# Linear attention and a gated feed-forward on one core: the queries' projections in two PSUM banks of their own, their third pass queued behind the next group's first, two stacked operands

## The chip, the cores and the metric

The kernel runs on one core of a Trainium2 chip. The metric is the device time of one launch in microseconds (us). Lower is better. The times before are the median of three runs, and one further execution was recorded by the hardware profiler.

The core's engines are called as the profile calls them: PE (TensorE, matrix products; PEld is its weight loader), DVE (VectorE), ACT (ScalarE), POOL (GpSimd) and SP (SyncE, which here only issues DMAs). Each engine works through its own list of instructions in the order in which they stand there, and an instruction that has to wait holds back all that stand behind it on that engine.

## The reference

```python
def phi(x):                                   # x: (8, 8, 576, 64), w_phi: (64, 128)
    proj = np.einsum('bhsd,df->bhsf', x, w_phi)
    proj = proj - np.max(np.abs(proj), axis=-1, keepdims=True)
    return np.concatenate([np.exp(proj), np.exp(-proj)], axis=-1)
q_p, k_p = phi(q), phi(k)
kv  = np.einsum('bhsf,bhsd->bhfd', k_p, v)
z   = np.sum(k_p, axis=2)
num = np.einsum('bhsf,bhfd->bhsd', q_p, kv)
den = np.einsum('bhsf,bhf->bhs', q_p, z)[..., None] + 1e-06
x   = num / den                               # heads side by side: (8, 576, 512)
h   = np.maximum(x @ w_in, 0.0)               # (8, 576, 1024)
conv = sum(conv_w[k] * shifted(h, k - 1) for k in range(3))
out = (h * sigmoid(conv)) @ w_out             # (8, 576, 512), all float32
```

## The kernel before

The eight batches are cut into two units each (four heads to a unit), and each unit into five groups of columns; group 0 has 128 columns of each of two heads, the others 256. Three kinds of process run through this list. A key process (`k_process`) projects a group of keys (PSUM tile `kp`), takes the largest absolute value and the exponentials, and adds the products with the values into `kv`. A query process (`q_process`) projects a group of queries (PSUM tile `qp`), takes the exponentials in both signs and multiplies them with `kv` (PSUM tile `nm`). The feed-forward process multiplies with `w_in` (`hp`), convolves, gates, and multiplies with `w_out` (`op`). A small planner at the end of the file steps these processes in turn. It decides in which order the instructions are traced; then a list scheduler, which holds a model of the engines, fixes each engine's list. The names in a list read as tile, batch, unit, group, and a running number: `qp5_0_1_6607` is the projection of batch 5, unit 0, group 1.

From batch 2 on a group of queries goes this way. Its columns are loaded by two DMAs on SP (`qr`, line 196). ACT copies them, rounded, into the stacked operand `qx` (line 199), and POOL puts the remainder into its lower half (line 200): rows 0 to 63 of `qx` are the rounded part, rows 64 to 127 the rest. PE makes a first and a second pass over `qx` into the PSUM tile `qp` (lines 353 and 354). The largest absolute value of each column is then found: by a reduction with a transpose on DVE (`qmt`, line 358), three small copies on ACT (line 361), and four small instructions on DVE (lines 365 to 369, `mx` and `qmp`). The negative maximum is brought back into two rows of `qx`, as a rounded part and its rest, by two DMAs on SP (line 371). A third pass on PE (line 378) subtracts it from `qp`. Only then can ACT take the two exponentials (line 387, `qe`), which free the bank of `qp`; the third pass is the last reader of `qx`, and frees its slot.

The first two batches go without the stack: their projections (line 220, also called `qp`) are normalised on DVE and turned by PE into the tile `tp` (line 346).

PSUM has eight banks here. The pool `pg` holds four under one tag `g`, which `qp`, `tp`, `kp` and `nm` share. The pool `pm` holds two (`hp`, `op`), and `pk` two for `kv`. A tile that asks for a bank waits until the last reader of an earlier tile is through: DVE's subtraction `ks` (line 230) for a `kp`, ACT's copies `num` (line 439) for an `nm`, ACT's exponentials for a `qp`. Of the stacked operand there are three slots (tag `qs`), of the tiles `num`, in which a unit's products are gathered, three. POOL also makes the keys' two parts (`kxh`, line 62, and `kxl`, line 65) and the first tap of the convolution (`c`, line 512).

Of the kernel before, what the change touches and what calls it, by code (L numbers as in the profile page):

```python
# [7 lines left out]
F32 = mybir.dt.float32  # L8
F32R = mybir.dt.float32r
# [3 lines left out]
ALU = mybir.AluOpType  # L13
AX = mybir.AxisListType.X

B, H, S, D = 8, 8, 576, 64
F = 128
DM, FF = 512, 1024
P = 128
# [3 lines left out]
VW = D + 1  # L23
# [12 lines left out]
def kernel(  # L36
# [150 lines left out]
    def load_split(src, b, qd, g, kind):  # L187
# [5 lines left out]
        if kind == "q":  # L193
            raw = sb.tile([P, 2, n * P], F32, name=f"qr{b}_{qd}_{g}", tag="qr", bufs=2)
            for h in range(2):
                nc.sync.dma_start(out=raw[D * h : D * h + D, :, :],
                                  in_=src[b, qd, :, c0 : c0 + n * P].rearrange("(i d) s -> d i s", d=D))
            x = sb.tile([P, 2, n * P], F32R, name=f"qx{b}_{qd}_{g}", tag="qs", bufs=3)
            nc.scalar.activation(out=x, in_=raw, func=AF.Copy)  # L199
# [9 lines left out]
    def project(n, hi, lo, b, qd, g, kind):  # L209

        if b == 0 and kind == "k":

            ps = pm.tile([P, n * 256], F32, name=f"{kind}p{b}_{qd}_{g}", tag="m")
        else:
            ps = pg.tile([P, n * 256], F32, name=f"{kind}p{b}_{qd}_{g}", tag="g", bufs=4)
        for t in range(n):
# [11 lines left out]
        nc.vector.tensor_reduce(out=m, in_=ps3, axis=AX, op=ALU.max, apply_absolute_value=True)  # L228
        pr = sb.tile([P, 2 * n, F], F32, name=f"{kind}s{b}_{qd}_{g}", tag=kind + "s", bufs=3 if kind == "q" else 2)
        nc.vector.tensor_tensor(out=pr, in0=ps3, in1=m.unsqueeze(2).broadcast_to([P, 2 * n, F]), op=ALU.subtract)  # L230
# [89 lines left out]
    den = {}  # L320
    numt = {}
    xh, xl = {}, {}

    def q_process(b, qd, g):
# [11 lines left out]
        if lo is None:  # L336
# [5 lines left out]

            tp = pg.tile([P, 2, n, P], F32, name=f"tp{b}_{qd}_{g}", tag="g", bufs=4)
            for t in range(n):
# [3 lines left out]
        else:  # L348
            x = hi
            tp = pg.tile([P, 2, n, P], F32, name=f"qp{b}_{qd}_{g}", tag="g", bufs=4)  # L350
            tpf, xf = tp.rearrange("p i t s -> p (i t s)"), x.rearrange("p i s -> p (i s)")
            c = w // 32
            nc.tensor.matmul(out=tpf, lhsT=wq_hi, rhs=xf, start=True, stop=False, skip_group_check=True)
            nc.tensor.matmul(out=tpf, lhsT=wq_lo, rhs=xf, start=False, stop=False, skip_group_check=True)

            mt = sb.tile([P, 4, 16], F32, name=f"qmt{b}_{qd}_{g}", tag="qmt", bufs=2)
            with tc.high_priority():
# [8 lines left out]
                nc.vector.tensor_reduce(out=m[:, 0:c], in_=mr, axis=AX, op=ALU.max)  # L366
                nc.vector.tensor_tensor(out=mp[:, 16 : 16 + c].bitcast(F32R), in0=m[:, 0:c], in1=mp[:, 0:c], op=ALU.subtract)
                mpt = sb.tile([32, 32], F32, name=f"qmp{b}_{qd}_{g}", tag="qmp", bufs=2)
                nc.vector.transpose(out=mpt, in_=mp)
                for i in range(2):  # L370
                    nc.sync.dma_start(out=xf[D + i : D + i + 1, :].bitcast(F32).rearrange("k (c t) -> k c t", t=32),
                                      in_=mpt[16 * i : 16 * i + c, :])
            yield pe(230 * n)
# [3 lines left out]
            with tc.high_priority():  # L377
                nc.tensor.matmul(out=tpf, lhsT=wq_m, rhs=xf, start=False, stop=True, skip_group_check=True)
            yield pe(115 * n)
# [15 lines left out]
        for pr_, _, _, _ in parts:  # L395
            if b > 0:
                yield until(("x", b - 1, qd * 2 + pr_, 1))
        ps = pg.tile([VW, 2, n * P], F32, name=f"nm{b}_{qd}_{g}", tag="g", bufs=4)
        ins = None
# [27 lines left out]
        for pr_, o, s0, w in parts:  # L427
            if (b, qd, pr_) not in den:
                den[b, qd, pr_] = sb.tile([72, 16], F32, name=f"den{b}_{qd}_{pr_}", tag="den", bufs=3)
                numt[b, qd, pr_] = sb.tile([P, S], F32, name=f"num{b}_{qd}_{pr_}", tag="num", bufs=3)  # L430
            dn, nt = den[b, qd, pr_], numt[b, qd, pr_]
# [271 lines left out]
```

## Time and profile before

| | |
|---|---|
| median of 3 runs | 848.88 us (848.18 to 851.27) |
| profiled execution | 846.93 us |
| its span, first to last instruction | 845.1 us |
| mean granted TensorE clock | 0.982 |
| PE busy | 784.7 us, 93% of the span |
| PEld busy | 746.8 us, 88% |
| DVE busy | 654.0 us, 77% |
| ACT busy | 637.9 us, 75% |
| POOL busy | 313.8 us, 37% |

The span is the time from the first instruction to the last, and what lies around it is 1.8 us. Busy time of an engine is the union of its instructions; matmuls overlap in the records, so that a PE row of 0.30 us can stand every 0.13 us. "Idle before" is the time in which the engine had nothing in it just before the instruction, and the name behind the arrow is the instruction that ended the wait.

### The profile page before, as it was taken

What the parts mean: (1) busy time and instruction counts of PE and PEld (TensorE: products, weight loads), DVE (VectorE), ACT (ScalarE), POOL (GpSimd) and SP (SyncE); (2) the same over time, 40 slices, a digit from 0 to 9 for tenths busy, and PEclk for the clock granted to TensorE, in tenths of its full rate; (3) what the DMA queues carried; (4) which work ended last, traced back from release to release, by engine and by line L of the source; (5) the groups of instructions that cost most, each with busy time, mean ns of one, the idle gap of its engine ahead of it and who ended that gap; (6) DMA issues with size and microseconds to landing.
All of it is one profiled execution on the core that took longest, in us unless ns stands there. A gap on an engine that the chain in (4) does not pass through costs nothing.

```text
span 845.1 us, 17785 instructions
## 1 busy us (share of the span) xinstructions
PE 784.7 (93%) x5972; PEld 746.8 (88%) x5972; DVE 654.0 (77%) x1570; ACT 637.9 (75%) x1468; POOL 313.8 (37%) x395
## 2 busy tenths in 40 slices
PE   7789789789989989998999999999989899999998
PEld 6678779789889979998999998998979889999998
DVE  6689997897887859887769887787868877766561
ACT  4689776979788788887889879799777978744332
POOL 5755564351533415334343342514515212211110
PEclk9999899999999999999999999999999999999999
DMA  5544322212121211222222322213212200000001
GB/s 167 159 135 136 115 77 55 83 30 81 55 85 44 84 40 51 71 70 71 69 78 55 88 55 86 56 47 92 57 48 58 73 21 11 22 30 29 23 15 50
DMA packets 68427, 56.49 MB, mean 67 GB/s; under 512 B 19440, under 2 KB 66288, under 8 KB 68336
## 3 DMA queue, kind: packets, MB, share of 16 engines
q1 hardware_dynamic: 68336, 55.36, 22.6%
q8 instruction: 48, 0.79, 0.4%
q14 instruction: 43, 0.35, 0.1%
HBM read 45.21 MB, written 9.44 MB: 65 GB/s over the span
## 4 chain that ended last, share of the span: by engine, by line
PE 54%; ACT 18%; DVE 13%; DMA 7%; issue 5%; SPq 2%; POOL 2%; ACTq 0%; DVEq 0%; POOLq 0%
PE op L548 16%; PE hp L489 16%; PE kv L279 7%; PE nm L416 6%; DVE c L517 3%; PE nm L408 2%; ACT qh L60 2%; ACT qe L387 2%; ACT num L439 2%; DVE ql L65 2%; ACT qx L199 1%; DMA qr<-in_qT_dram 1%; DMA w_r<-in_w_in_dram 1%; ACT c L521 1%; PE qp L220 1%
## 5 line engine op out<-in xcount | busy, mean ns | idle before, releaser
L512 POOL TENSOR_SCALAR c<-h,cw 128x288 f32<-128x288 f32 x128 | 87.4, 686 | 229.5 <-ACT h L496 192.9
L517 DVE SCALAR_TENSOR_TENSOR c<-h,cw,c 128x287 f32<-128x287 f32 (+1 forms) x256 | 138.5, 548 | 38.0 <-POOL c L512 36.5
L279 PE MATMUL kv<-v,ke 128*128 128x65 f32 x1024 | 159.4, 254 | 3.2 <-ACT ke L260 3.2
L279 PEld LDWEIGHTS kv<-v,ke 128*128 128x128 f32 x1024 | 154.2, 193 | 8.3 <-ACT ke L260 3.8
L489 PE MATMUL hp<-xh,win_hi 128*128 128x290 f32 x512 | 155.9, 306 | 3.6 <-ACT os L553 1.4
L489 PE MATMUL hp<-xl,win_hi 128*128 128x290 f32 x512 | 155.1, 303 | 0.0
L489 PE MATMUL hp<-xh,win_lo 128*128 128x290 f32 x512 | 154.3, 301 | 0.0
L548 PE MATMUL op<-gh,wout_hi 128*128 128x288 f32 x512 | 152.2, 298 | 0.5 <-ACT os L553 0.5
L548 PE MATMUL op<-gl,wout_hi 128*128 128x288 f32 x512 | 151.6, 296 | 0.0
L548 PE MATMUL op<-gh,wout_lo 128*128 128x288 f32 x512 | 151.4, 296 | 0.0
L200 POOL TENSOR_TENSOR qx<-qr,qx 64x512 fp32r<-64x512 f32 (+1 forms) x60 | 77.6, 1296 | 137.6 <-ACT qx L199 99.0
L65 DVE TENSOR_TENSOR ql<-qe,qh 128x512 fp32r<-128x512 f32 x112 | 92.3, 838 | 28.3 <-ACT qh L60 28.0
L489 PEld LDWEIGHTS hp<-xh,win_hi 128*128 128x128 f32 x512 | 98.3, 193 | 8.0 <-ACT os L553 3.3
L489 PEld LDWEIGHTS hp<-xl,win_hi 128*128 128x128 f32 x512 | 99.3, 194 | 1.2 <-DVE den L452 0.2
L489 PEld LDWEIGHTS hp<-xh,win_lo 128*128 128x128 f32 x512 | 99.1, 194 | 0.4
L548 PEld LDWEIGHTS op<-gh,wout_hi 128*128 128x128 f32 x512 | 96.2, 188 | 2.0 <-ACT os L553 1.2
L548 PEld LDWEIGHTS op<-gh,wout_lo 128*128 128x128 f32 x512 | 96.5, 188 | 0.3
L548 PEld LDWEIGHTS op<-gl,wout_hi 128*128 128x128 f32 x512 | 96.3, 188 | 0.5
L496 ACT ACTIVATE h<-hp 128x290 f32<-128x290 f32 x128 | 51.5, 407 | 38.4 <-PE hp L489 37.7
L62 POOL TENSOR_SCALAR kxh<-kr 128x256 fp32r<-128x256 f32 (+1 forms) x80 | 41.3, 518 | 103.1 <-PE kp L224 72.1
L416 PE MATMUL nm<-ql,kvh 128*65 128x256 f32 x224 | 68.8, 309 | 1.1 <-DVE ql L65 0.8
L416 PE MATMUL nm<-qh,kvh 128*65 128x256 f32 x224 | 62.6, 287 | 7.0 <-ACT num L439 4.4
(99 smaller groups left out, 1905.8 us busy)
## 6 DMA issues: line engine op xcount, KB each, us to landing
qr<-in_qT_dram SPq DMA_DIRECT2D x112, 128.0 KB
v<-in_vt_dram SPq DMA_DIRECT2D x80, 130.0 KB
out_dram<-os SPq DMA_DIRECT2D x64, 144.0 KB
kr<-in_kT_dram SPq DMA_DIRECT2D x64, 128.0 KB
w_r<-in_w_in_dram SPq DMA_DIRECT2D x8, 512.0 KB
w_r<-in_w_out_dram SPq DMA_DIRECT2D x8, 512.0 KB
rr<-rc SPq DMA_DIRECT2D x128, 2.2 KB
qr<-in_qT_dram SPq DMA_DIRECT2D x28, 64.0 KB
```

The lines of the kernel that those rows point to most:

```text
L60: nc.scalar.activation(out=hi, in_=src, func=AF.Copy)
L62: nc.gpsimd.tensor_scalar(out=hi, in0=src, scalar1=1.0, scalar2=0.0, op0=ALU.mult, op1=ALU.add)
L65: eng_lo.tensor_tensor(out=lo, in0=src, in1=hi.bitcast(F32), op=ALU.subtract)
L200: nc.gpsimd.tensor_tensor(out=x[D:P], in0=raw[D:P], in1=x[D:P].bitcast(F32), op=ALU.subtract)
L279: ins = nc.tensor.matmul(out=kp[i][:, s, p0 : p0 + VW], lhsT=lhsT, rhs=v[:, (2 * t + i) * VW : (2 * t + i + 1) * VW], start=False, stop=(g ...
L387: nc.scalar.activation(out=e, in_=tps, func=AF.Exp, scale=1.0 - 2.0 * s)
L416: ins = after(ins, lambda: nc.tensor.matmul(out=ps[:, i, o : o + w], lhsT=w_, rhs=x_, start=(k == 0), stop=(k == 5)))
L489: nc.tensor.matmul(out=ps, lhsT=w_, rhs=x_, start=(k == 0), stop=(k == 11))
L496: nc.scalar.activation(out=hs, in_=ps, func=AF.Relu)
L512: nc.gpsimd.tensor_scalar(out=cv, in0=hs[:, o : o + TC], scalar1=cw[:, f, 1:2], scalar2=0.0, op0=ALU.mult, op1=ALU.add)
L517: nc.vector.scalar_tensor_tensor(out=cv[:, lo:hi], in0=hs[:, o + j - 1 + lo : o + j - 1 + hi], scalar=cw[:, f, j : j + 1], in1=cv[:, lo:hi ...
L548: nc.tensor.matmul(out=ps, lhsT=w_, rhs=x_, start=(k == 0), stop=(k == 23))
```

## The change

Five edits go together. The four shared PSUM banks become two with the tag `gq`, which only the queries' `qp` and `tp` use, and two with the tag `g` for `kp` and `nm`. The third pass of a group is bound to stand behind the first pass of the next group in PE's list. This is an edge for the scheduler's order alone and adds no semaphore. The two rows of the maximum are laid side by side (`mp[:, c : 2 * c]` in place of `mp[:, 16 : 16 + c]`) and go in one DMA, not two. The slots with the tag `qs`, the stacked operands and the first batches' normalised projections, are two, not three. The tiles `num` are four, not three. The instructions of PE, DVE, ACT and POOL are the same in kind and number.

```diff
--- before.py
+++ after.py
@@ -195,7 +195,7 @@
             for h in range(2):
                 nc.sync.dma_start(out=raw[D * h : D * h + D, :, :],
                                   in_=src[b, qd, :, c0 : c0 + n * P].rearrange("(i d) s -> d i s", d=D))
-            x = sb.tile([P, 2, n * P], F32R, name=f"qx{b}_{qd}_{g}", tag="qs", bufs=3)
+            x = sb.tile([P, 2, n * P], F32R, name=f"qx{b}_{qd}_{g}", tag="qs", bufs=2)
             nc.scalar.activation(out=x, in_=raw, func=AF.Copy)
             nc.gpsimd.tensor_tensor(out=x[D:P], in0=raw[D:P], in1=x[D:P].bitcast(F32), op=ALU.subtract)
             return n, x, x
@@ -212,7 +212,7 @@
 
             ps = pm.tile([P, n * 256], F32, name=f"{kind}p{b}_{qd}_{g}", tag="m")
         else:
-            ps = pg.tile([P, n * 256], F32, name=f"{kind}p{b}_{qd}_{g}", tag="g", bufs=4)
+            ps = pg.tile([P, n * 256], F32, name=f"{kind}p{b}_{qd}_{g}", tag="gq" if kind == "q" else "g", bufs=2)
         for t in range(n):
             o = ps[:, t * 256 : (t + 1) * 256]
             his = hi[:, t * P : (t + 1) * P]
@@ -226,7 +226,7 @@
         ps3 = ps.rearrange("p (t f) -> p t f", f=F)
         m = sb.tile([P, 2 * n], F32, name=f"{kind}m{b}_{qd}_{g}", tag="m", bufs=4)
         nc.vector.tensor_reduce(out=m, in_=ps3, axis=AX, op=ALU.max, apply_absolute_value=True)
-        pr = sb.tile([P, 2 * n, F], F32, name=f"{kind}s{b}_{qd}_{g}", tag=kind + "s", bufs=3 if kind == "q" else 2)
+        pr = sb.tile([P, 2 * n, F], F32, name=f"{kind}s{b}_{qd}_{g}", tag=kind + "s", bufs=2)
         nc.vector.tensor_tensor(out=pr, in0=ps3, in1=m.unsqueeze(2).broadcast_to([P, 2 * n, F]), op=ALU.subtract)
         return pr
 
@@ -319,6 +319,13 @@
 
     den = {}
     numt = {}
+    firsts, third = {}, {}
+
+    def behind(ins, other):
+
+        tc.add_manual_dep(ins.ins, other.ins.name,
+                          mybir.DependencyInfo(mybir.DependencyClass.NoSync, mybir.DependencyReason.DATA),
+                          reason="a group's third pass behind the next group's first")
     xh, xl = {}, {}
 
     def q_process(b, qd, g):
@@ -340,17 +347,20 @@
             yield until(back("num", 2))
             set_ready(("tp", *divmod(j, 5)))
 
-            tp = pg.tile([P, 2, n, P], F32, name=f"tp{b}_{qd}_{g}", tag="g", bufs=4)
+            tp = pg.tile([P, 2, n, P], F32, name=f"tp{b}_{qd}_{g}", tag="gq", bufs=2)
             for t in range(n):
                 for i in range(2):
                     nc.tensor.transpose(out=tp[:, i, t, :], in_=pr[:, 2 * t + i, :], identity=idn)
             yield pe(220 * n)
         else:
             x = hi
-            tp = pg.tile([P, 2, n, P], F32, name=f"qp{b}_{qd}_{g}", tag="g", bufs=4)
+            tp = pg.tile([P, 2, n, P], F32, name=f"qp{b}_{qd}_{g}", tag="gq", bufs=2)
             tpf, xf = tp.rearrange("p i t s -> p (i t s)"), x.rearrange("p i s -> p (i s)")
             c = w // 32
-            nc.tensor.matmul(out=tpf, lhsT=wq_hi, rhs=xf, start=True, stop=False, skip_group_check=True)
+            first = nc.tensor.matmul(out=tpf, lhsT=wq_hi, rhs=xf, start=True, stop=False, skip_group_check=True)
+            firsts[j] = first
+            if j - 1 in third:
+                behind(third.pop(j - 1), first)
             nc.tensor.matmul(out=tpf, lhsT=wq_lo, rhs=xf, start=False, stop=False, skip_group_check=True)
 
             mt = sb.tile([P, 4, 16], F32, name=f"qmt{b}_{qd}_{g}", tag="qmt", bufs=2)
@@ -364,18 +374,18 @@
                 mr = mt[0:32, :, 0:c].rearrange("p a c -> p c a")
                 nc.vector.tensor_reduce(out=mp[:, 0:c].bitcast(F32R), in_=mr, axis=AX, op=ALU.max)
                 nc.vector.tensor_reduce(out=m[:, 0:c], in_=mr, axis=AX, op=ALU.max)
-                nc.vector.tensor_tensor(out=mp[:, 16 : 16 + c].bitcast(F32R), in0=m[:, 0:c], in1=mp[:, 0:c], op=ALU.subtract)
+                nc.vector.tensor_tensor(out=mp[:, c : 2 * c].bitcast(F32R), in0=m[:, 0:c], in1=mp[:, 0:c], op=ALU.subtract)
                 mpt = sb.tile([32, 32], F32, name=f"qmp{b}_{qd}_{g}", tag="qmp", bufs=2)
                 nc.vector.transpose(out=mpt, in_=mp)
-                for i in range(2):
-                    nc.sync.dma_start(out=xf[D + i : D + i + 1, :].bitcast(F32).rearrange("k (c t) -> k c t", t=32),
-                                      in_=mpt[16 * i : 16 * i + c, :])
+                nc.sync.dma_start(out=xf[D : D + 2, :].bitcast(F32).rearrange("k (c t) -> k c t", t=32), in_=mpt[0 : 2 * c, :])
             yield pe(230 * n)
             yield wait(4000)
             yield until(back("num", 2))
             set_ready(("tp", *divmod(j, 5)))
             with tc.high_priority():
-                nc.tensor.matmul(out=tpf, lhsT=wq_m, rhs=xf, start=False, stop=True, skip_group_check=True)
+                third[j] = nc.tensor.matmul(out=tpf, lhsT=wq_m, rhs=xf, start=False, stop=True, skip_group_check=True)
+            if j + 1 in firsts:
+                behind(third.pop(j), firsts[j + 1])
             yield pe(115 * n)
         f32 = 2 * b + qd < NKV_F32 or g == 0
         qh = sb.tile([P, 2, 2, n * P], F32 if f32 else F32R, name=f"qh{b}_{qd}_{g}", tag="qh", bufs=2)
@@ -395,7 +405,7 @@
         for pr_, _, _, _ in parts:
             if b > 0:
                 yield until(("x", b - 1, qd * 2 + pr_, 1))
-        ps = pg.tile([VW, 2, n * P], F32, name=f"nm{b}_{qd}_{g}", tag="g", bufs=4)
+        ps = pg.tile([VW, 2, n * P], F32, name=f"nm{b}_{qd}_{g}", tag="g", bufs=2)
         ins = None
         for pr_, o, s0, w in parts:
             for i in range(2):
@@ -427,7 +437,7 @@
         for pr_, o, s0, w in parts:
             if (b, qd, pr_) not in den:
                 den[b, qd, pr_] = sb.tile([72, 16], F32, name=f"den{b}_{qd}_{pr_}", tag="den", bufs=3)
-                numt[b, qd, pr_] = sb.tile([P, S], F32, name=f"num{b}_{qd}_{pr_}", tag="num", bufs=3)
+                numt[b, qd, pr_] = sb.tile([P, S], F32, name=f"num{b}_{qd}_{pr_}", tag="num", bufs=4)
             dn, nt = den[b, qd, pr_], numt[b, qd, pr_]
 
             dro = dr[D : D + 1, 2 * o : 2 * (o + w)]
```

The change moves instructions in every list. On PE, at the passage from unit 0 of batch 4 to batch 5, two third passes stood next to each other before, with the next group's first pass behind them; the names in square brackets are the engines or DMA queues whose semaphores the row waits for:

```order
L378 MATMUL qp4_1_4_6338<-qx4_1_4_5827,wq_m_80 128x512 [waits DMAHW7_49,DMAHW5_49]
L378 MATMUL qp5_0_0_6369<-qx5_0_0_5943,wq_m_80 128x256 [waits DMAHW6_49,DMAHW0_49,DVE_49]
L223 MATMUL kp5_1_0_6596<-wbd_hi_72,kxh5_1_0_6387 128x256 [waits PE_49,Activation_49,Pool_49]
L224 MATMUL kp5_1_0_6596<-wbd_lo_73,kxh5_1_0_6387 128x256
L225 MATMUL kp5_1_0_6596<-wbd_hi_72,kxl5_1_0_6388 128x256 [waits Pool_49]
L353 MATMUL qp5_0_1_6607<-qx5_0_1_6396,wq_hi_78 128x512 [waits DVE_49]
L354 MATMUL qp5_0_1_6607<-qx5_0_1_6396,wq_lo_79 128x512
```

The same place on PE in the changed kernel, where line 360 is the first pass, 364 the second and 386 the third:

```order
L223 MATMUL kp5_1_0_6565<-wbd_hi_72,kxh5_1_0_6356 128x256 [waits DVE_49,PE_49,Pool_49]
L224 MATMUL kp5_1_0_6565<-wbd_lo_73,kxh5_1_0_6356 128x256
L225 MATMUL kp5_1_0_6565<-wbd_hi_72,kxl5_1_0_6357 128x256 [waits Pool_49]
L360 MATMUL qp5_0_1_6576<-qx5_0_1_6365,wq_hi_78 128x512 [waits Pool_49]
L386 MATMUL qp5_0_0_6339<-qx5_0_0_5914,wq_m_80 128x256 [waits DMAHW7_49]
L364 MATMUL qp5_0_1_6576<-qx5_0_1_6365,wq_lo_79 128x512
```

The third pass of group 0 now stands between the first and the second pass of group 1. The first pass waits for POOL, which makes its operand, where it waited for DVE, which freed its bank.

On POOL, in unit 1 of batch 4, the remainders of two groups (line 200) stood next to each other before:

```order
L200 TENSOR_TENSOR qx4_1_2_5661<-qr4_1_2_5658,qx4_1_2_5661 64x512 [waits DMAHW4_49,DMAHW2_49,DMAHW7_49,Activation_49,Pool_49]
L200 TENSOR_TENSOR qx4_1_3_5821<-qr4_1_3_5818,qx4_1_3_5821 64x512 [waits DMAHW5_49,DMAHW2_49,DMAHW6_49,PE_49,Activation_49]
L62 TENSOR_SCALAR kxh5_0_3_5934<-kr5_0_3_5932 128x256 [waits DMAHW6_49,PE_49,Pool_49]
L65 TENSOR_TENSOR kxl5_0_3_5935<-kr5_0_3_5932,kxh5_0_3_5934 128x256 [waits PE_49,Pool_49]
L512 TENSOR_SCALAR c6_6405<-h6_0_5959,cw_95 128x288 [waits DVE_49,Activation_49]
```

The same stretch of POOL's list in the changed kernel, where the first tap of the convolution has line 522:

```order
L200 TENSOR_TENSOR qx4_1_2_5635<-qr4_1_2_5632,qx4_1_2_5635 64x512 [waits PE_49,DMAHW0_49,Activation_49,Pool_49]
L62 TENSOR_SCALAR kxh5_0_3_5905<-kr5_0_3_5903 128x256 [waits DMAHW2_49,PE_49,Pool_49]
L65 TENSOR_TENSOR kxl5_0_3_5906<-kr5_0_3_5903,kxh5_0_3_5905 128x256 [waits PE_49,Pool_49]
L200 TENSOR_TENSOR qx4_1_3_5793<-qr4_1_3_5790,qx4_1_3_5793 64x512 [waits DMAHW3_49,PE_49,DMAHW4_49,Activation_49,Pool_49]
L522 TENSOR_SCALAR c6_6374<-h6_0_5930,cw_95 128x288 [waits DVE_49,Activation_49,Pool_49]
L200 TENSOR_TENSOR qx4_1_4_5799<-qr4_1_4_5796,qx4_1_4_5799 64x512 [waits DMAHW0_49,DMAHW2_49,Activation_49,Pool_49]
```

The remainder of group 3 moved behind the next keys' two instructions, and that of group 4 came between two taps of the convolution: each is now made for the group that comes next, none a group ahead.

In PE's lists of the two kernels, counted in matmuls over the 60 groups: between the first passes of neighbouring groups lie 25 matmuls or fewer in 20 of 59 cases before and in none after (the least is 33). From a group's third pass to the first pass of the group after the next lie between -58 (the first pass stands ahead) and 113 before, and between 26 and 58 after, 42 in the middle. From a group's first to its third pass lie at least 61 before, 51 after, and 80 in the middle in both.

## The prediction

> **What bounds the kernel now.** I read the page's first part, then the busy times by stage, because the page's shares mix three stages with different limits. The three stretches are the first two batches (with the loading of the weights), the batches in which queries go through the stacked operand, and the tail without attention.
>
> ```profile
> span 845.1 us, 17785 instructions
> core 0: us, PE busy (x) PEld busy (x) DVE busy (x) ACT busy (x) POOL busy (x), PEclk, DMA share, GB/s
> 0.00:150.00 150.00, 126.97 (x875) 113.72 (x876) 126.57 (x240) 109.36 (x235) 85.39 (x107) 0.93 0.41 121
> 150.00:706.00 556.00, 522.38 (x4090) 498.81 (x4089) 445.07 (x1128) 462.28 (x1090) 210.59 (x255) 0.99 0.22 62
> 706.00:845.00 139.00, 135.33 (x1011) 134.28 (x1009) 82.36 (x204) 66.23 (x145) 17.79 (x34) 1.00 0.08 27
> ```
>
> The tail is PE's alone, idle 3.7 us, and the change touches nothing in it. In the middle stage PE is busy 522.4 of 556.0 us. ACT with 462.3 (83%) and DVE with 445.1 (80%) are behind it, so PE sets the pace, and what can be gained there is its 33.6 us of idle time. That is at most 4% of the kernel. Next I asked who ends PE's waits in that stretch (engine, line, what it waited for: us in total, times, longest).
>
> ```profile
> PE nm L416 <- ACT num L439: 4.4, 5, 2.1
> PE qp L353 <- issue: 3.7, 3, 1.6
> PE qp L353 <- POOL qx L200: 3.4, 4, 1.2
> PE qp L378 <- DMA qx<-qmp: 3.3, 5, 1.7
> PE kp L223 <- issue: 2.8, 2, 2.3
> PE qp L353 <- DVE ks L230: 1.9, 4, 0.8
> PE kp L223 <- ACT num L439: 1.8, 1, 1.8
> PE qp L353 <- ACT qe L387: 1.7, 2, 1.3
> PE kp L223 <- DVE ks L230: 1.0, 1, 1.0
> PE qp L353 <- ACT num L439: 0.9, 1, 0.9
> PE kp L223 <- ACT qe L387: 0.8, 2, 0.4
> PE qp L353 <- POOL kxh L62: 0.5, 1, 0.5
> PE nm L416 <- ACT qh L387: 0.2, 1, 0.2
> ```
>
> The same waits by the waiting line, for the first and the third pass:
>
> ```profile
> L353 PE MATMUL qp<-qx,wq_hi 128*128 128x512 f32 (+1 forms) x59 | 24.1, 409 | 12.4 <-issue 3.7 <-POOL qx L200 3.4 <-DVE ks L230 1.9
> L378 PE MATMUL qp<-qx,wq_m 128*128 128x512 f32 (+1 forms) x59 | 23.2, 401 | 3.3 <-DMA qx<-qmp 3.3
> ```
>
> The reader should see that the first pass is the costliest place: 12.4 of the 33.6 us stand before line 353. Four causes of it (DVE's `ks`, ACT's `num` and `qe`, "issue") are what a wait for a bank looks like. Only `qx` is a wait for the operand. The third pass costs 3.3 us more.
>
> **Part 1: the banks.** A first pass that has a bank of the queries' own no longer waits for keys (`ks`) or products (`num`). Of its 12.4 us I leave what is not such a wait: 3.4 for `qx`, 0.5 for `kxh`, and 1.7 for `qe`, since the queries' own exponentials still free its bank. That takes 12.4 - 5.6 = 6.8 us off, 3.7 of it under "issue", which the trace does not explain. I count those as bank waits because between neighbouring first passes, where one of them had to wait, lay 25 matmuls or fewer in 20 of 59 cases, and now lie 33 or more. Keys and products no longer wait for a query's bank either: 0.8 (`kp` for `qe`) and 0.2 (`nm` for `qh`) go, 1.0 us. Together -7.8 us; without the "issue" rows it would be -4.1, and with the `qe` rows too -9.5.
>
> In return `kp` and `nm` have two banks instead of a share in four. What they wait for among themselves is 4.4 + 1.8 + 1.0 + 2.8 = 10.0 us now. I take no change: two queries' tiles sat in the common four for most of the time already, from first pass to exponentials, 80 matmuls and more. The bounds are -5 (half of it goes) and +10 (it doubles). Perfetto Trace Analysis, in the Trainium skill, section Optimizing Tensor Performance, advises rotating independent groups of matmuls through different banks, so that reading one out overlaps the next; that speaks against narrowing either kind to two. The rows above agree that a bank's release is what PE waits for, and by the rule the waits of `kp` and `nm` would grow; that outcome is the fourth case below.
>
> In the first two batches `qp` and `tp` share the two banks of the queries, and the normalised projections have two slots. PE waits there for a bank or a slot at these rows, of that stretch:
>
> ```profile
> PE qp L220 <- issue: 2.6, 1, 2.6
> PE tp L346 <- ACT num L439: 1.8, 1, 1.8
> PE nm L416 <- ACT qe L387: 1.4, 1, 1.4
> PE qp L220 <- ACT qh L387: 1.4, 2, 0.8
> ```
>
> DVE is at 126.6 of 150 us there and hides most of what PE does. I take 0 between -4 (the rows but `tp`'s own go, in part) and +4 (as much is added).
>
> **Part 2: the order of the third pass.** It adds no instruction and, on the chip, no semaphore. What can cost is that a late third pass stands ahead of the next group's second pass, or that an early one waits its turn. The chain that a third pass waits for is built from these rows:
>
> ```profile
> L358 DVE TRANSPOSE_TENSOR_REDUCE qmt<-qp x60: 401/702/719, 152.3 to 706.4; 128x16 f32<-128x512 f32 x48, 128x8 f32<-128x256 f32 x12
> L361 ACT ACTIVATE qmt<-qmt x180: 206/213/217, 153.6 to 708.2; 32x16 f32<-32x16 f32 x144, 32x8 f32<-32x8 f32 x36
> L371 SPq DMA_DIRECT2D qx<-qmp x120: 502/580/721, 158.2 to 714.3; - x120
> L387 ACT ACTIVATE qe<-qp x96: 569/594/622, 182.0 to 721.2; 128x512 f32<-128x512 f32 x96
> L199 ACT ACTIVATE qx<-qr x60: 399/631/651, 142.2 to 699.3; 128x512 fp32r<-128x512 f32 x48, 128x256 fp32r<-128x256 f32 x12
> L200 POOL TENSOR_TENSOR qx<-qr,qx x60: 728/1287/2042, 142.7 to 700.1; 64x512 fp32r<-64x512 f32 x48, 64x256 fp32r<-64x256 f32 x12
> ```
>
> First pass to third pass is 80 matmuls in the middle in both lists. PE starts one of them about every 0.13 us, as in this run of twelve (11 steps in 1.46 us):
>
> ```profile
> 307.54 0.30 PE L548 MATMUL op<-gh,wout_hi 128*128 128x288 f32 x1
> ...
> 309.00 0.29 PE L548 MATMUL op<-gh,wout_lo 128*128 128x288 f32 x1
> ```
>
> That is 10.6 us of cover; the shortest distance falls from 61 matmuls (8.1 us) to 51 (6.8 us). I price the move itself at 0; part 3 has its gain, and the shorter cover is the risk to it.
>
> **Part 3: one DMA, not two.** Sixty issues of 0.58 us (line 371) leave SP. SP is not on PE's path as a rule, but here the second issue stood directly between `qmp` and the third pass. The third pass waited 5 times for this DMA, 3.3 us in all; a start 0.58 us earlier takes 5 x 0.58 = 2.9 us off. The bounds are 0, if one transfer of two rows lands later than two of one row, and -3.3. The same page of the Trainium skill, section DMA Optimizations, says that splitting DMAs can let the work complete sooner when the DMA engines are mostly idle, and they are at 0.22 here. By that rule this term would be 0, and the sum 2.9 us higher. I stay with -2.9, as line 371's own issue time is measured and the landing of 2 KB is not likely to differ by as much.
>
> **Part 4: two stacked operands.** With three slots ACT and POOL could make a group's `qx` long before its turn. With two, line 199 for group j+2 can only start when group j's third pass is done. Behind that pass now come, in series, the pass itself (0.40), two exponentials (2 x 0.594, which stand ahead on ACT as a rule), the copy (0.63) and POOL's remainder (1.29): 3.5 us before the first pass of group j+2. The list gives 42 matmuls in the middle, 5.6 us, and 26 at the least, 3.4 us. So about 2 us are spare for what else is queued on ACT, which is 83% busy, and on POOL. POOL itself already waits for ACT's copy more than for anything else in this chain:
>
> ```profile
> POOL qx L200 <- ACT qx L199: 93.3, 30, 17.1
> ```
>
> Before, 4 first passes waited for `qx`, 0.85 us each. I take one in six now: 10 x 0.85 = 8.5, which is +5.1 us over the 3.4 there are. The spare 2 us are three ACT instructions, and I judge that more than three are queued about that often. The lower bound is 0 (nothing added). The upper is half of all first passes, 30 x 0.85 = 25.5, or +22 us. POOL's list behind line 200 (`kxh`, `kxl`, `c`) is held back with it; keys have slack there, as POOL is 38% busy (210.6 of 556).
>
> **Part 5: the rest.** Four `num` tiles remove waits of ACT's line 439 for a slot, of which the list of waits shows none: 0. The maximum's other place is the same instruction on DVE: 0, nothing to hide.
>
> **The sum.** -7.8 (banks) -2.9 (DMA) +5.1 (operand) = -5.6 us against the profiled execution's 846.93, so 841.3. The median of the runs stands 1.95 above the profiled one; with that, 843.3 us.
>
> **The rivals.** A run's time can tell about 0.5% from no change, 4.2 us, which puts the borders at 844.6 and 853.1.
>
> The first case is the sum: 843.3, own range 836 to 844.6. For it speaks that the largest single group of PE's waits is the one that the edit addresses.
>
> The second: the waits only move. DVE and ACT are at 80 and 83%, and PE's idle time ahead of line 353 lets them catch up; taken away there, it reappears at `nm` (line 416) or `hp`, because the engine that makes the next operand is no faster. Then the 10.7 us of gain shrink to what the operand costs, 5.1: near 848, with 844.6 to 853.1 as its band. The number of causes that each hold under 2 us speaks for it.
>
> The third is slower: the two stacked operands close a loop. Third pass, ACT, POOL, first pass, reduction, DMA, third pass has two groups in it and no reserve, so each delay on ACT reaches PE. At half of all first passes, +22 instead of +5.1, the sum is 846.93 - 10.7 + 22 + 1.95, about 860. It decides from 3.4 + 10.7 = 14.1 us of waiting for `qx` on, 17 of 60 first passes. The 42 matmuls of cover speak against it, ACT's 83% for it.
>
> The fourth: keys and products lack banks. If their 10.0 us of waits triple, the sum is 20 higher, 863. That a key's bank is free again after two DVE instructions speaks against it.
>
> That the change does not do what it says is excluded: in the new list all 59 third passes stand behind the next first pass.
>
> **How the numbers follow.** I give the first case 0.43, the second 0.30, the third 0.18, the fourth 0.09. Faster by over 0.5% is the first, 0.43; within 0.5% the second, 0.30; slower the last two, 0.27. The likeliest gives 843.3. A range of 8 in 10 takes the first but for the tail under 835, the second, and the nearer half of the third: 835 to 858.
>
> **What would show it.** After, in the middle stage: line 360's waits for `ks` and `num` gone and its idle time under 12.4 us, with POOL's `qx` as its main cause at about 8.5 us; line 386's wait for the DMA near 0.4 us; `kp` and `nm` waiting about 10 us as before; PE's idle in the stage near 28 us. The prediction is wrong if line 360 waits over 14 us for `qx`, if `kp` and `nm` wait over 20, or if the waits of line 360 fall and PE's idle time in the stage stays at 33 us all the same.

## The result and the profile after

The changed kernel takes 835.5 us in the median of four runs (835.33 to 837.11), the kernel before 848.84 us in four runs beside it. The ratio is 0.984, with a 95% interval of 0.982 to 0.987: 13.3 us faster, where 5.6 were forecast. The direction and the likeliest case (faster by over 0.5%) are right. The size is more than twice the sum, half a microsecond inside the low end of the range and as much below the first case's own range of 836 to 844.6.

Not all of the 13.3 us is in the two traces. The profiled execution of the changed kernel is the slowest of its four (837.11), that of the kernel before lies 1.9 us under its median. So the traces differ by 9.8 us, and the other 3.5 are the place of each profiled run among its fellows. The page after, and its busy times by stage (same columns as before):

```profile
span 835.3 us, 17596 instructions
PE 781.6 (94%) x5972; PEld 746.7 (89%) x5972; DVE 666.5 (80%) x1570; ACT 635.3 (76%) x1468; POOL 310.3 (37%) x395
```

```profile
core 0: us, PE busy (x) PEld busy (x) DVE busy (x) ACT busy (x) POOL busy (x), PEclk, DMA share, GB/s
0.00:150.00 150.00, 130.12 (x887) 115.92 (x888) 130.87 (x243) 111.47 (x241) 86.59 (x108) 0.94 0.42 122
150.00:706.00 556.00, 526.93 (x4163) 507.49 (x4162) 460.48 (x1144) 464.31 (x1098) 206.13 (x256) 0.99 0.22 62
706.00:835.00 129.00, 124.53 (x925) 123.26 (x925) 75.17 (x185) 59.55 (x131) 17.61 (x32) 1.00 0.08 28
```

PE's idle time fell by 4.5 us in the middle stage (33.6 to 29.1), by 3.1 in the first two batches (23.0 to 19.9), and rose by 0.8 in the tail; PE's busy time is 3.1 lower. The list of PE's waits in the middle stage, which answers to the one in the prediction:

```profile
PE qp L386 <- DMA qx<-qmp: 5.7, 7, 1.6
PE qp L360 <- POOL qx L200: 4.7, 5, 1.6
PE kp L223 <- ACT num L449: 4.0, 3, 2.9
...
PE hp L499 <- ACT os L563: 2.4, 4, 0.8
PE nm L426 <- DVE ql L65: 2.0, 3, 0.9
PE nm L426 <- ACT qh L60: 1.8, 3, 1.1
...
PE kp L223 <- DVE ks L230: 1.3, 2, 1.1
PE nm L426 <- ACT num L449: 1.2, 3, 0.6
...
PE nm L426 <- DVE ks L230: 0.3, 1, 0.3
PE qp L360 <- issue: 0.3, 1, 0.3
```

The first pass (line 360, 353 before) no longer waits for `ks`, `num` or `qe`; its idle time is 5.0 us, not 12.4. The third pass (line 386) waits longer than before, 5.7 us and not 3.3. The sum foresaw the first and had the second at 0.4.

### The profile page after: what moved, and what is told of

The parts are those of the page before. It is cut to its first block, busy times and chain, and to the rows that moved or that the text cites. A ratio compares the mean times of both kernels' runs of the same rounds, so it can differ in the third digit from the quotient of the medians.

```text
span 835.3 us, 17596 instructions
## 1 busy us (share of the span) xinstructions
PE 781.6 (94%) x5972; PEld 746.7 (89%) x5972; DVE 666.5 (80%) x1570; ACT 635.3 (76%) x1468; POOL 310.3 (37%) x395
## 4 chain that ended last, share of the span: by engine, by line
PE 32%; ACT 13%; DVE 9%; issue 4%; DMA 4%; POOL 1%; SPq 1%; ACTq 0%; POOLq 0%; DVEq 0%
PE op L558 12%; PE hp L499 11%; PE nm L426 3%; PE kv L279 3%; DVE c L527 2%; ACT qe L397 2%; DMA den<-dr 2%; ACT qh L60 1%; DVE ql L65 1%; ACT gh L60 1%; ACT dr L444 1%; ACT num L449 1%; ACT qx L199 1%; ACT c L531 1%; ACT L397 1%
## 5 line engine op out<-in xcount | busy, mean ns | idle before, releaser
L279 PEld LDWEIGHTS kv<-v,ke 128*128 128x128 f32 x1024 | 157.2, 195 | 10.6 <-ACT ke L260 3.4
L279 PE MATMUL kv<-v,ke 128*128 128x65 f32 x1024 | 163.6, 256 | 2.4 <-ACT ke L260 2.2
L527 DVE SCALAR_TENSOR_TENSOR c<-h,cw,c 128x288 f32<-128x288 f32 (+1 forms) x256 | 143.8, 572 | 26.2 <-POOL c L522 24.6
L499 PE MATMUL hp<-xl,win_hi 128*128 128x290 f32 x512 | 152.9, 299 | 0.0
L499 PE MATMUL hp<-xh,win_lo 128*128 128x290 f32 x512 | 152.5, 298 | 0.0
L522 POOL TENSOR_SCALAR c<-h,cw 128x288 f32<-128x288 f32 x128 | 81.5, 640 | 183.5 <-ACT h L506 145.0
L200 POOL TENSOR_TENSOR qx<-qr,qx 64x512 fp32r<-64x512 f32 (+1 forms) x60 | 75.5, 1258 | 162.8 <-ACT qx L199 144.5
L65 DVE TENSOR_TENSOR ql<-qe,qh 128x512 fp32r<-128x512 f32 x112 | 86.5, 788 | 27.0 <-ACT qh L60 26.8
L65 DVE TENSOR_TENSOR gl<-c,gh 128x288 fp32r<-128x288 f32 x128 | 55.5, 485 | 22.6 <-ACT gh L60 22.5
```

What stands on the lines that cost most here:

```text
L65: eng_lo.tensor_tensor(out=lo, in0=src, in1=hi.bitcast(F32), op=ALU.subtract)
L200: nc.gpsimd.tensor_tensor(out=x[D:P], in0=raw[D:P], in1=x[D:P].bitcast(F32), op=ALU.subtract)
L279: ins = nc.tensor.matmul(out=kp[i][:, s, p0 : p0 + VW], lhsT=lhsT, rhs=v[:, (2 * t + i) * VW : (2 * t + i + 1) * VW], start=False, stop=(g ...
L499: nc.tensor.matmul(out=ps, lhsT=w_, rhs=x_, start=(k == 0), stop=(k == 11))
L522: nc.gpsimd.tensor_scalar(out=cv, in0=hs[:, o : o + TC], scalar1=cw[:, f, 1:2], scalar2=0.0, op0=ALU.mult, op1=ALU.add)
L527: nc.vector.scalar_tensor_tensor(out=cv[:, lo:hi], in0=hs[:, o + j - 1 + lo : o + j - 1 + hi], scalar=cw[:, f, j : j + 1], in1=cv[:, lo:hi ...
```

## Experiments

Each run has its own kernel-before runs on the same chip, and the ratio is to those. Runs are named by their number.

### One edit undone, lists free (1 to 4)

Run 1 is the changed kernel without the edge in the order.

```diff
             firsts[j] = first
-            if j - 1 in third:
-                behind(third.pop(j - 1), first)
...
-            if j + 1 in firsts:
-                behind(third.pop(j), firsts[j + 1])
```

> The changed kernel without the edge that puts the third pass behind the next group's first; all else as changed. If the banks are the gain (first theory), the order edge is worth nothing and the time stays at 835 to 837. If the even spacing of the first passes is the gain (second theory), two queries' banks alone let the pairs come back and it returns to 843 to 849, with line 360 waiting over 8 us again. If the gain is only that the scheduler happened on a better list (third theory), it lies anywhere from 833 to 849 and no wait explains it.

Measured: 0.998 (0.995 to 1.001). Without the edge nearly the whole gain is gone, 11.6 us of it, though the edge adds no semaphore. PE's longest wait in it:

```profile
PE kp L223 <- ACT num L445: 10.0, 8, 3.5
```

Run 2 gives the four banks back their one tag.

```diff
-..., tag="gq" if kind == "q" else "g", bufs=2)     # projections
+..., tag="g", bufs=4)
-..., tag="gq", bufs=2)                             # tp, qp
+..., tag="g", bufs=4)
-..., tag="g", bufs=2)                              # nm
+..., tag="g", bufs=4)
```

> The changed kernel with one tag of four banks for queries, keys and products, as before; the order edge, the one DMA and the two stacked operands stay. First theory: the gain of the banks goes, 845 to 850, with the first pass waiting again for DVE's ks and ACT's num. Second theory: the edge spaces the first passes by itself, 835 to 839. Third: anywhere.

Measured: 1.018 (1.014 to 1.023). With two operands and shared banks the first pass does wait for its operand, above the 14.1 us at which the third case of the prediction decides:

```profile
PE qp L360 <- POOL qx L200: 18.9, 15, 2.2
```

Run 3 has three operand slots again, and three `num` tiles, since a third slot beside four of them does not fit.

```diff
-            x = sb.tile([P, 2, n * P], F32R, name=f"qx{b}_{qd}_{g}", tag="qs", bufs=2)
+            x = sb.tile([P, 2, n * P], F32R, name=f"qx{b}_{qd}_{g}", tag="qs", bufs=3)
-        pr = sb.tile([P, 2 * n, F], ..., tag=kind + "s", bufs=2)
+        pr = sb.tile([P, 2 * n, F], ..., tag=kind + "s", bufs=3 if kind == "q" else 2)
-                numt[...] = sb.tile([P, S], ..., tag="num", bufs=4)
+                numt[...] = sb.tile([P, S], ..., tag="num", bufs=3)
```

> The changed kernel with three slots for the stacked operand and, since SBUF has no room for both, three num tiles. By the prediction's step the operand's waits cost about 5 us, so this would be 830 to 832 and the first pass's wait for POOL's qx falls from 4.7 us in the profile to under 1. If those waits only stand in place of others, it stays at 835 to 837.

Measured: 0.993 (0.990 to 0.995), 7 us slower than the changed kernel and outside both expectations. Its operand waits are nearly gone, and others stand in their place, of which "issue" is the largest:

```profile
PE qp L360 <- issue: 8.4, 4, 3.7
PE kp L223 <- ACT num L449: 7.1, 4, 2.9
...
PE qp L360 <- POOL qx L200: 1.0, 1, 1.0
```

Run 4 has two DMAs again.

```diff
-                ...(out=mp[:, c : 2 * c]...
-                nc.sync.dma_start(out=xf[D : D + 2, :]..., in_=mpt[0 : 2 * c, :])
+                ...(out=mp[:, 16 : 16 + c]...
+                for i in range(2):
+                    nc.sync.dma_start(out=xf[D + i : D + i + 1, :]..., in_=mpt[16 * i : 16 * i + c, :])
```

> The changed kernel with the two rows of the maximum in two DMAs again. By the prediction's step this costs 2.9 us: 838 to 839, with line 386's wait for the DMA up from 5.7 us in the profile by 3 or more. If the second issue is hidden: 835 to 837.

Measured: 1.014 (1.011 to 1.017), 25 us slower than the changed kernel for 60 small issues. At the prediction's price, 0.58 us at each third pass that waits for this DMA (11 here), the issues come to 6 us. In these four kernels the scheduler had made other lists for every engine, so each run mixes the edit with another order of all the work.

### The DMA with the lists held (5, 6)

For the next two, the list of every engine is held. A table of the order in which another kernel's engines work is put behind the program, and each instruction is tied to the one ahead of it by an edge for the scheduler alone:

```python
for engine, at in LISTS.items():          # order of the other kernel, by number of tracing
    made = [i for i in instructions if i.engine == engine]
    for x, y in zip(at, at[1:]):
        tc.add_manual_dep(made[y], made[x].name, NoSync, ...)
```

In the traces, PE's matmuls of each run with held lists (5, 6, 13, 14, 17) stand in the order of the kernel that the list was taken from, one by one. A run that holds a list and changes nothing else was not made.

Run 5 is the changed kernel with two DMAs as in run 4, and the changed kernel's lists.

> The changed kernel with the maximum's two rows in two DMAs again, and every engine's list held word for word to that of the changed kernel (a table of the lists is tied to the instructions by order edges; on SP the second DMA stands right behind the first). In the run with two DMAs and free lists the time went to 861. If the second DMA itself is what cost that, this stays near 860. If it is the lists that the scheduler then made, this is the changed kernel plus what the issue costs, 835 + 0 to 4: 836 to 839.

Measured: 0.992 (0.989 to 0.994). So of run 4's 25 us, 6.2 (give or take 3) are the second DMA, and about 19 the lists. The third pass of run 5 against the 5.7 us of the changed kernel:

```profile
PE qp L388 <- DMA qx<-qmp: 11.8, 12, 2.1
```

Run 6 is the kernel before with one DMA and its own lists.

> The kernel before with the maximum's two rows in one DMA, and every engine's list held word for word to that of before (on SP the one DMA stands at the first one's place). By the prediction's step the DMA alone gives 2.9 us: 846. If its worth is only in the lists: 848 to 850.

Measured: 0.994 (0.991 to 0.996), 5.3 us faster. By groups, the first and the third pass of run 6:

```profile
L353 PE MATMUL qp<-qx,wq_hi 128*128 128x512 f32 (+1 forms) x60 | 24.3, 405 | 6.9 <-issue 2.0 <-DVE ks L230 1.6 <-POOL qx L200 1.6
...
L376 PE MATMUL qp<-qx,wq_m 128*128 128x512 f32 (+1 forms) x60 | 23.5, 400 | 1.5 <-DMA qx<-qmp 1.4
```

The third pass waits 1.8 us less (3.3 to 1.5), which is what the prediction had in mind. But the first pass waits 5.5 less (12.4 to 6.9), with the same banks and the same order. An earlier third pass also frees bank and operand earlier, and everything behind it on PE can come sooner. That this is the cause was not tried, and this trace is no clean measure of it: its execution is the slowest of the run's nine (846.46 us), and in the middle stage PE is busy 530.3 us at a clock of 0.97, not 522.4 at 0.99. Part of the shorter waits can come from that. Of the 5.5 us, 1.7 stood under "issue", 1.8 under `qx`, and 0.3 to 0.6 under each of `ks`, `qe`, `num` and `kxh`.

### Other draws of the lists (7, 8, 11, 12, 18)

To see how far lists alone move the time, the planner's reach `AHEAD` was set to other numbers. It decides in which order the work is traced, and changes no resource.

```diff
-AHEAD = 300
+AHEAD = 310        # 7: before; 8: changed; 12: run 3's kernel.  11: changed, 330.  18: changed, 290
```

> The kernel before with the scheduler's head start for attention from 310 in place of 300: no instruction, bank or slot is another, only the lists shuffle (1300 lines of PE's list differ). If the time hangs on the waits that the prediction counted, 847 to 851. If the lists are a lottery (third theory), it moves by more than 4 us either way.

> The changed kernel with the same number 310 in place of 300 (1658 lines of PE's list differ). If the banks and the order edge are the gain, 833 to 839. If the changed kernel is one lucky list, it goes up by more than 4 us, to between 840 and 860.

> The changed kernel with AHEAD 330 in place of 300: nothing but the order of the lists differs. With 310 it was 0.989. First theory (the gain is of the resources): 0.980 to 0.990. Third theory (the changed kernel's lists are a lucky draw): the draws centre near 0.990, so 0.986 to 0.998 here.

> The changed kernel with three operand slots and three num tiles, and AHEAD 310: another draw of the lists of the kernel with three operands, which gave 0.993 at 300. First theory (three operands are worse by 0.9% in any order): 0.990 to 1.000, slower than the changed kernel's at the same AHEAD (0.989). Third theory: 0.984 to 0.998, as likely below 0.989 as above.

> The changed kernel with AHEAD 290, a fourth draw of its lists. The three so far gave 0.984, 0.989 and 0.993. If the changed kernel's list is a draw like others: 0.984 to 0.996, most likely near 0.989. If the resources bring all of it: 0.980 to 0.988.

| kernel | AHEAD 290 | 300 | 310 | 330 |
|---|---|---|---|---|
| before | | 1 | 0.995 (0.993 to 0.997) | |
| changed | 0.995 (0.992 to 0.997) | 0.984 (0.982 to 0.987) | 0.989 (0.986 to 0.992) | 0.993 (0.989 to 0.996) |
| run 3's (three operands, three `num`) | | 0.993 (0.990 to 0.995) | 0.989 (0.987 to 0.992) | |

The changed kernel's own list is the best of four. The other three average 0.992. The 7 us by which three operands seemed worse do not survive another draw: at 310 the two kernels are equal.

### Operands and `num`: the resource or the list (9, 10, 13, 14, 16)

Run 9 is the changed kernel with three `num` tiles and all else as changed (the last pair of run 3's diff alone), run 16 the same at `AHEAD` 310. Run 10 is the kernel before with two operand slots (the first two pairs of run 3's diff, the other way).

> The changed kernel with three tiles num, not four; all else as changed. It separates the fourth num tile from the two operands, which went back together in the kernel with three operands (ratio 0.993). First theory (two operands with the order's edge and own banks space the groups evenly, and num is worth nothing, as the prediction said): ratio 0.980 to 0.989, as the changed kernel's 0.984. Second theory (the fourth num tile brought the 0.9%): about 0.993, with line 449's num as a cause of PE's waits above 10 us. Third theory (each edit moves the scheduler's lists, which scatter by 0.5% either way): anywhere from 0.979 to 0.995.

> The changed kernel with three num tiles and AHEAD 310: another draw of its lists. If the fourth num tile is worth 1.3% as a resource, the ratio is 0.995 to 1.003 (the changed kernel gave 0.989 at 310). If it was the draw, 0.984 to 0.993.

> The kernel before with two operand slots in place of three and nothing else changed. The prediction's operand term by itself: +5.1 us, ratio 1.006, with line 353 waiting about 8.5 us for qx; its third case: +22 us, ratio 1.026. First theory (two operands only pay with own banks and the edge): 1.006 to 1.026, since a shared bank delays a first pass and so the third pass that frees the slot. Third theory (lists scatter): 0.995 to 1.005, with waits for qx under 5 us.

Measured: run 9, 0.997 (0.995 to 0.999); run 16, 0.999 (0.997 to 1.002); run 10, 1.022 (1.020 to 1.024). By itself run 9 says that the fourth tile is worth 11 us, and run 10 that the loop of two operands, with shared banks, costs 18.5. Runs 13 and 14 hold the lists of runs 10 and 9, and give the resource back: the third slot, the fourth tile. If the chip had waited for it, the time would come back.

> The kernel before, with its three operand slots, but with every engine's list pinned to that of the kernel with two operands alone (1.022). If the 18 us are waits for a slot, giving the third slot back takes off the 12.8 us of line 353's waits for qx and most of what follows from them: ratio 0.998 to 1.008. If they are the scheduler's other lists, the waits for qx fall little and the ratio stays at 1.015 to 1.024.

> The changed kernel, with its four num tiles, but with every engine's list pinned to that of the kernel with three num tiles (0.997). If those 11 us are waits of ACT or PE for a num tile, the ratio falls to 0.984 to 0.988. If they are the lists, it stays at 0.994 to 1.000.

Measured: run 13, 1.023 (1.019 to 1.026); run 14, 0.997 (0.995 to 0.999). Nothing came back, in either. The first pass of run 10 and of run 13, by groups, one fence each:

```profile
L353 PE MATMUL qp<-qx,wq_hi 128*128 128x512 f32 (+1 forms) x60 | 24.3, 404 | 18.8 <-POOL qx L200 12.8 <-ACT num L439 1.8 <-DVE ks L230 1.7
```

```profile
L353 PE MATMUL qp<-qx,wq_hi 128*128 128x512 f32 (+1 forms) x60 | 24.4, 407 | 19.4 <-POOL qx L200 12.9 <-DVE ks L230 2.4 <-ACT num L439 1.8
```

The wait for `qx` is the same with two slots and with three. So it is no wait for a slot. In run 10's list of waits, ACT's line 199 never waits for a third pass, which is what frees a slot. What changed is where the scheduler put ACT's and POOL's work on `qx`. From the end of line 200 to the first pass, the trace has a median of 8.6 us before, 1.5 in run 10, 1.4 in run 13 and 1.5 in the changed kernel. The lists that the scheduler made for two slots have the operand finished just before its turn, and the third slot cannot undo that. The waits for a `num` slot in run 9 are one row of ACT's list, 1.4 us of the 11:

```profile
ACT num L449 <- DVE xf L476: 1.4, 2, 0.9
```

Taken one at a time, with banks, edge and one DMA in place and free lists, the two edits have the same sign at both numbers. Two operands for three cost 3.7 us at 300 (run 9 against run 3) and 8.7 at 310 (run 16 against run 12). The fourth `num` tile then brings 11.0 (the changed kernel against run 9) and 9.0 (run 8 against run 16). As a pair they come to -7.3 and to 0. The first pass's wait for `qx` goes with the operands: it is 4.6 to 7.9 us in the six kernels of this kind with two (the changed one, 8, 9, 11, 16, 18), and at most 1.0 in the three with three (3, 12, 17). Each difference has an interval of some 3 us, and rests on single lists.

### Banks and edge alone (15, 17)

Run 15 is the kernel before with the queries' own banks and the edge, lists free. Run 17 adds the one DMA, with run 15's lists.

> The kernel before with the queries' own banks and the order's edge, and with two DMAs, three operands and three num tiles. The prediction's banks term: -7.8 us, ratio 0.991, with line 360's waits for issue, ks and num gone. From the kernel with three operands (0.993) less the one DMA (0.6 to 0.7%): about 1.000, with a line of waits at 223 and 426 that has taken over what line 360 no longer waits. Scatter of the lists: 0.5% either way of that.

> Own banks and the order's edge, three operands and three num tiles, one DMA in place of two, and every engine's list pinned to that of the kernel with banks and edge alone (0.994). If the one DMA is worth the same at every list (0.62% and 0.73% at the two others): 0.986 to 0.989. If it is worth what that kernel's row of waits for it at the third pass shows, which is under 2 us: 0.992 to 0.995.

Measured: run 15, 0.994 (0.993 to 0.996), 4.8 us faster; run 17, 0.992 (0.989 to 0.994), 2.3 us more, but the two intervals overlap. In run 15 the third pass has little to wait for, as its waits show among those of PE:

```profile
PE hp L501 <- ACT os L565: 7.6, 11, 1.6
PE kp L223 <- ACT num L451: 5.8, 4, 2.9
...
PE qp L360 <- issue: 3.9, 5, 1.3
...
PE qp L360 <- POOL kxh L62: 1.6, 1, 1.6
...
PE qp L388 <- DMA qx<-qmp: 1.0, 4, 0.3
```

The first pass waits 5.6 us by groups and not 12.4, for neither `ks` nor `num` nor `qe`. In the same kernel `hp` waits 7.6 us for `os` (1.4 before) and `kp` 5.8 for `num` (1.8 before). Part of the gain has moved there. Run 15's 4.8 us are one list against one list; the kernel before, shuffled, gains 4.2 with no edit at all (run 7). So the rows show what banks and edge do at the first pass, but that they bring 4.8 us is not shown.

## Why the prediction was right in direction and wrong in size

The step that failed lies under all five parts of the sum: it read the waits of the one list that there was and took the new lists as the old ones less some waits. What the scheduler would make anew was put at nothing, without a reason. In the sum's terms, the fourth `num` tile stood at 0 and came out at -11.0 and -9.0 in two draws, all of it by way of the lists in the one that was tried (run 14). And the operands' +5.1 did not come through as a loss, since in neither draw did the two edits together cost anything.

Put in one row, from runs on free and on held lists: banks and edge -4.8 us (run 15), one DMA -2.3 more (run 17), operands and `num` about 0 (run 17's 0.992 against the changed kernel's three other draws, 0.992 on average), the changed kernel's own list -6.5 (0.984 against those three). That sums to -13.6 against the 13.3 measured. Each step has an interval of 1.4 to 2.7 us either way, and the scatter of the lists besides, so it is a budget and not four exact numbers; the steps also compare different lists. With all lists free at 300 the same way reads -4.8, -1.3 (run 3 against run 15), +3.7 (two operands) and -11.0 (`num`).

**The banks (-7.8 forecast, -4.8 with the edge in one draw).** The mechanism is as told: the waits for `ks`, `num` and `qe` at the first pass are gone, 12.4 to 5.0 us in the changed kernel. Mis-sized were two things in it. The 3.7 us under "issue" were counted as waits for a bank, but with banks of the queries' own there are still 3.9 (run 15) and 8.4 (run 3) of them. And of the 6.8 us that were given to the banks at the first pass, 2.5 ("issue", `ks`, `num`) go with one DMA alone in run 6's trace, so they need not be the banks'. What the second rival feared, that the waits move, came in part. In run 15 `hp` and `kp` wait about 10 us more. In the changed kernel's middle stage `nm` waits 4.7 us for its own operands (`ql`, `qh`, `gh`; 1.1 before), `hp` and `op` wait 5.3 (2.5 before), and the third pass 2.4 more. So line 360 lost 7.4 us, and the bank waits of `kp` and `nm` 4.2 (11.0 to 6.8, with the 1.0 that part 1 counted apart), but PE's idle time in the stage only 4.5.

`kp` and `nm` did not pay for their two banks: 4.0 + 1.3 + 1.2 + 0.3 = 6.8 us in the stage after, against 10.0. The fourth case falls. From the Trainium skill's advice to rotate matmul groups through different banks (Perfetto Trace Analysis, Optimizing Tensor Performance) the prediction had drawn that these waits would grow with two banks per kind; here the measured rows decide.

**The DMA (-2.9 forecast; -5.3, -6.2 and -2.3 at three lists).** The term was mis-sized. It priced the 0.58 us of the issue at the five third passes that waited. Two things were missing. In run 6's trace the first pass's waits fall three times as much as the third's, with the reservation made there. And the second issue did not always follow at once: in the trace before it started 0.62 us behind the first in the median, but 3.0 to 3.8 us behind in 3 of 60. Worked out from the runs' intervals, run 6 has 3.1 to 7.4 us, so the forecast's upper bound of 3.3 lies at the very end of what that list allows. The rule of the Trainium skill that was weighed (Perfetto Trace Analysis, DMA Optimizations: split transfers may let the work finish sooner when the DMA engines are mostly idle) would have made this term 0, as the prediction read it. For two rows of at most 2 KB each, with the engines at 0.22, runs 5 and 6 say otherwise.

**The operands (+5.1 forecast; +3.7 and +8.7 by themselves, about 0 with the fourth `num` tile).** The size is near, the reasoning is not. It took the loop third pass, ACT, POOL, first pass as a wait on the chip. In the changed kernel `qx` costs 4.7 us (5 waits, where 10 at 0.85 were forecast), 1.3 more than before, and ACT's line 199 waits once for a third pass. The loop is closed ahead of time, in the list: `qx` is planned late, and then waited for. Something of the third rival's size did come, +15.6 us in run 2 and +18.5 in run 10, with `qx` as the largest wait. For run 10, run 13 shows that it is the list: it stays when the slot is given back. For run 2 and for the changed kernel that was not tried.

**The `num` tiles (0 forecast; -11.0 and -9.0).** The prediction looked for waits of ACT's line 439 for a slot, found none and wrote 0. On the chip that is right: with three tiles there are 1.4 us of such waits (run 9), and giving the fourth back to that list brings nothing (run 14). But the scheduler makes other lists when it has four, and the time is in these.

**What the sum had no term for.** The prediction read the waits of one list, and then took the new lists as the old ones less some waits. Edits that change no resource move this kernel by 0.5 to 1% (runs 7, 8, 11, 18), as much as the whole forecast. The changed kernel's list is 6.5 us better than the average of its three siblings. That term has no sign that the profile of before could give. With an average list the change would have measured 0.992, 842 us, close to the 843.3 forecast; but that rests on three draws, and part of it on errors that cancel. The kernel before has a list of its own too, and not its best (0.995 at 310): the average of its two draws and that of the changed kernel's four lie 6 us apart. That this is near the 5.6 forecast is luck as much as skill. Two reservations stay. The changed kernel itself was measured in four executions at one time and not again beside its siblings. And the traces do not show the 6.5 us: the profiled executions of the changed kernel, run 8 and run 11 took 837.1, 837.0 and 838.3 us, with 29.1, 29.7 and 28.6 us of PE's idle time in the middle stage.

**What would show it.** Right: line 360 under 12.4 with `qx` as main cause; `kp` and `nm` no worse; PE's idle in the stage 29.1 (28 forecast). Wrong: `qx` at 4.7 (8.5 forecast), and the third pass's wait at 5.7 (0.4 forecast). By the runs it goes with the two operands rather than with the edge: 8.3 in run 10 without the edge, 1.0 in run 15 with the edge and three operands, and 11.8 in run 5 without the one DMA. The sum counted the middle stage's idle time, and there -5.6 stands against -4.5 in the traces. The rest of the gap lies where it had nothing: 3.1 us of PE's idle time in the first two batches (0 was taken, between -4 and +4), 3.1 of its busy time, less 0.8 in the tail, and the 3.5 between profiles and medians, as the 1.95 us that were added were no constant (after, it is -1.6).

**Open.** Banks and edge were not tried with lists held, neither together nor one without the other. Run 1, without the edge, falls back to 0.998, but on another list. Why the scheduler finds worse lists with two operands and three `num` tiles (runs 9 and 16) and not with three and three (runs 3 and 12) stays open, and what the waits under "issue" at the first pass are.

## What to carry to other kernels

Where a scheduler makes the lists, undoing an edit does not price it: hold the lists and change the resource (or give the scarce one back), and the chip's own part stands apart from the order's. Take several draws of the lists, of both kernels, before a gain of 1% is put down to an edit. A resource that the chip never waits for can still be worth something, because the scheduler plans with it. And look for what a step in a serial chain costs at everything that the end of the chain frees, not only at the place where the end itself waits.

## What the runs showed of the hardware that was not expected

A second issue on SP can cost more than the waits at its own reader show: with the lists held, leaving it out made run 6 faster by 5.3 us (3.1 to 7.4), where the third passes had waited 3.3 us for this DMA in all and still waited 1.4 after. And a slot that the chip does not wait for can still go with 18 us: with the third slot given back, the time stayed at 866.6 us, and the row of waits for `qx` at 12.9.
